# Other start addresses in SBUF for the weights and for the tiles that are multiplied with them

## The chip, the cores and the metric

The kernel runs on one core of a Trainium2 chip. The metric is the time of one execution on the device in microseconds (us). Three runs of the kernel before took 629.53, 631.18 and 634.5 us; their median is 631.18 us.

## The reference

Causal attention over 4 batches, 12 heads, 448 positions and a head size of 64, and behind it a layer of two matrices with a hardswish between them, on all 1792 positions. All is float32.

```python
scores = (1 / sqrt(64)) * matmul(q, k^T); scores = where(above diagonal, -1e9, scores)
attn = exp(scores - max); attn = attn / (sum(attn) + 1e-9)
x = heads of matmul(attn, v), side by side            # (1792, 768)
h = x @ w_in                                          # w_in  (768, 2048)
g = h * clip(h + 3, 0, 6) / 6
out = g @ w_out                                       # w_out (2048, 768)
```

## The kernel before

The 1792 positions are worked on in four groups of 448 columns. For each group attention gives x, transposed, as six tiles of 128 rows by 448 columns; the layer then computes h (16 tiles of 128 x 448) and out (6 tiles).

A float32 number is split into a high part, rounded to the type fp32r, and a low part, the remainder. One product of 128 x 128 weights with a 128 x 448 tile is then three matmuls, written in `triple` (lines 670 to 672): high weights with high data (L670), high weights with low data (L671), low weights with high data (L672). Each loads its own 128 x 128 weights first (the records named LDWEIGHTS) and then streams 448 columns past them. Weights are read from the tiles `wh` (high) and `wl` (low), in the last stage partly from `pr2`. The streamed operand is called the moving operand here. In the first product of each group, and in everything of the last stage, it is a tile of the pool `d` of shape [128, 2, 448], the high part in the first 1792 bytes of each partition and the low part in the next 1792. In the second product of the first two groups it is one of the 16 slots of `gh` (high) or `gl` (low), 1792 bytes each.

Groups 0 and 1 are computed one after the other (`group`), with the attention of later groups run in between. Groups 2 and 3 are computed together in the last stage (`last_first`, `last_second`) by a scheme with seven instead of eight block products, whose sums and differences DVE, POOL and ACT make. The attention's own products (L357, L414, L427, L500, L523 and L594 in plain float32, L502 and L503 in fp32r) lie in the first 400 us.

The order of the instructions on all engines is made by a planner in Python (`Flow`), which simulates the engines with fixed costs and does not know addresses. Every tile is then taken from a pool of equal slots, one pool per tag. The pools are laid out one behind the other in SBUF in the order of the table `BUFS`, so that the size of each pool decides where the next one starts:

```text
pool, start in bytes per partition, slot size x slots, start of a slot modulo 512
gh      21024  28672 x 1    32 (slot i of 1792 bytes: 32 for even i, 288 for odd i)
gl      49696  28672 x 1    32 (the same)
prow    78368     64 x 4
r       78624   1792 x 4    288, 32
kl      85792   1792 x 3    288, 32
vr      91168   2048 x 3    32
wh      97312   3072 x 3    32
wl     106528   3072 x 3    32
pr2    115744   1536 x 3    32
pr1    120352    896 x 3
wd     123040   4096 x 6    160
d      147616   3584 x 22   160 (high part); 1792 further on 416 (low part)
```

A weight tile of 128 columns is 512 bytes wide, so every 128 x 128 piece of `wh`, `wl` or `pr2` starts at the same address modulo 512. Lines 225 to 229 make the pools. `move` (L268) and `minus` (L280) are the helpers through which ACT, DVE and POOL make the high and low parts.

Of the kernel before, what the change touches and what calls it, by code (L numbers as in the profile page):

```python
# [9 lines left out]
F32 = mybir.dt.float32  # L10
# [28 lines left out]
    gh=1, gl=1, prow=4, r=4, kl=3, vr=3, wh=3, wl=3, pr2=3, pr1=3, wd=6, d=22,  # L39
)  # L40
BANKS = dict(b=8)

KINDS = dict(
    qk="d qk", op="d op", x="d x", pt="d pt", pr3="d pr3", xq="d xq", xc="d xc", gt="d gt", so="d so",
# [172 lines left out]
def tile_causal_attention_hardswish_moe(ctx: ExitStack, tc: tile.TileContext, q, k, v, w_in, w_out, out):  # L217
# [4 lines left out]
    kept_s = nc.dram_tensor("kept_s", (4, 2, 2, 128, HK, 256), F32).ap()  # L222
    kept_x = nc.dram_tensor("kept_x", (2, NPAIR, 128, S), F32).ap()

    pools = {}
    for tag, bufs in dict(const=1, **BUFS).items():
        pools[tag] = ctx.enter_context(tc.tile_pool(name=tag, bufs=bufs))
    for tag, bufs in BANKS.items():
        pools[tag] = ctx.enter_context(tc.tile_pool(name=tag, bufs=bufs, space=bass.MemoryType.PSUM))

    flow = Flow({**BUFS, **BANKS, **MOST})

# [849 lines left out]
```

## Time and profile before

| | |
|---|---|
| median of three runs | 631.18 us |
| the profiled execution, its own time | 632.49 us |
| its span, first to last instruction | 630.8 us |
| TensorE (PE) busy | 611.4 us, 97% |
| DVE, ACT, POOL busy | 502.7, 366.7, 279.9 us |
| mean granted TensorE clock | 0.984 of full speed |

A matmul's record begins when it starts and ends when its result is modelled to have left the array, so records of neighbouring matmuls overlap and their durations say nothing of the rate. The rate of TensorE is read from the starts: the time from the start of one matmul to the start of the next, called the pace here. The rows give starts to 0.01 us, so a pace is taken over many matmuls.

### The profile page before, as it was taken

The numbers are of one execution on the slowest core, as the hardware profiler recorded it, in microseconds if no ns is written. First come the engines' busy times: TensorE is split into PE (matmuls) and PEld (weight loads), VectorE is DVE, ScalarE is ACT, GpSimd is POOL, SyncE is SP. The second block draws the span as 40 slices with busy tenths as digits, with TensorE's granted clock in tenths as the row PEclk, the third lists the DMA queues.
The fourth block names the chain that finished last, engine by engine and source line by source line (L and its number), as shares of the span: only waits on it lengthen the run. The fifth ranks groups of instructions, "written<-read, shape, count | busy, mean of one in ns | idle before, by whom it ended". The sixth has DMA issues, their size and how long they took to land.

```text
span 630.8 us, 11229 instructions
## 1 busy us (share of the span) xinstructions
PE 611.4 (97%) x3636; PEld 526.7 (83%) x3636; DVE 502.7 (80%) x1060; ACT 366.7 (58%) x861; POOL 279.9 (44%) x274
## 2 busy tenths in 40 slices
PE   6879999999999999999999999999999999999997
PEld 5659797887887878779888788899999989999996
DVE  4998988897798665786998887498878888798851
ACT  3766666655545757667677655375555465446630
POOL 1667686464444434459377553015654453010000
PEclk8869999999999999999999999999999999999999
DMA  9979887787898444466477664335455367583311
GB/s 224 238 243 321 267 268 248 242 263 263 289 302 249 137 132 149 128 173 178 133 199 210 190 176 129 122 113 178 155 155 163 117 189 237 155 264 101 123 55 55
DMA packets 83578, 118.81 MB, mean 188 GB/s; under 512 B 22272, under 2 KB 59328, under 8 KB 83520
## 3 DMA queue, kind: packets, MB, share of 16 engines
q1 hardware_dynamic: 83520, 118.10, 61.7%
q8 instruction: 29, 0.48, 0.3%
q14 instruction: 29, 0.24, 0.1%
HBM read 90.93 MB, written 27.13 MB: 187 GB/s over the span
## 4 chain that ended last, share of the span: by engine, by line
PE 87%; DVE 5%; DMA 4%; SPq 1%; issue 1%; ACT 1%; POOL 0%; ACTq 0%; DVEq 0%
PE b L670 23%; PE b L672 22%; PE b L671 22%; PE b L523 7%; PE b L594 6%; PE b L500 5%; DMA gl<-in_v_dram 2%; DMA gh<-in_k_dram 1%; SPq L259 1%; PE b L502 1%; DVE d L280 1%; PE b L503 1%; DVE kl L280 1%; DVE b L555 1%; DVE gl L280 0%
## 5 line engine op out<-in xcount | busy, mean ns | idle before, releaser
L670 PE MATMUL b<-d,wh 128*128 128x448 f32 x504 | 189.3, 376 | 1.4 <-ACT r L268 1.1
L672 PE MATMUL b<-d,wl 128*128 128x448 f32 x504 | 185.1, 367 | 0.0
L671 PE MATMUL b<-d,wh 128*128 128x448 f32 x504 | 184.8, 367 | 0.0
L268 ACT CAST wh<-wd 128x768 fp32r<-128x768 f32 (+1 forms) x92 | 71.5, 778 | 59.5 <-PE b L671 39.1
L670 PEld LDWEIGHTS b<-d,wh 128*128 128x128 f32 x504 | 95.3, 189 | 11.7 <-ACT r L268 1.4
L672 PEld LDWEIGHTS b<-d,wl 128*128 128x128 f32 x504 | 95.1, 189 | 8.2
L671 PEld LDWEIGHTS b<-d,wh 128*128 128x128 f32 x504 | 95.3, 189 | 7.4
L280 DVE TENSOR_TENSOR wl<-wd,wh 128x768 fp32r<-128x768 f32 (+1 forms) x65 | 61.6, 947 | 30.2 <-ACT wh L268 30.0
L555 DVE CUSTOM_DVE_ANT_0 b<-b,mask 112x448 f32<-112x448 f32 (+2 forms) x144 | 69.7, 533 | 19.5 <-PE b L500 14.0
L280 POOL TENSOR_TENSOR wl<-wd,wh 128x768 fp32r<-128x768 f32 (+1 forms) x27 | 47.1, 1747 | 69.4 <-ACT wh L268 63.1
L268 ACT COPY d<-b 112x336 f32<-112x336 f32 (+3 forms) x137 | 55.7, 452 | 36.2 <-PE b L594 26.6
L280 POOL TENSOR_TENSOR wl<-d,wh 128x512 fp32r<-128x512 f32 (+1 forms) x38 | 58.2, 1534 | 39.8 <-ACT wh L268 37.6
L670 PE MATMUL b<-gh,wh 128*128 128x448 f32 x192 | 73.5, 383 | 0.0
L672 PE MATMUL b<-gh,wl 128*128 128x448 f32 x192 | 70.2, 365 | 0.0
L671 PE MATMUL b<-gl,wh 128*128 128x448 f32 x192 | 70.1, 365 | 0.0
L562 ACT ACTIVATE pr<-b,prow 112x336 f32<-112x336 f32 (+1 forms) x96 | 46.9, 495 | 7.7 <-PE b L594 4.8
L280 POOL TENSOR_TENSOR wd<-wd 128x256 f32<-128x256 f32 (+1 forms) x20 | 19.9, 1001 | 57.6 <-DMA wd<-kept_w 34.2
L523 PE MATMUL b<-d,vr 112*64 112x224 f32 (+2 forms) x504 | 44.9, 329 | 0.0
L523 PEld LDWEIGHTS b<-d,vr 112*64 112x64 f32 x504 | 30.6, 137 | 15.5 <-issue 2.8
L594 PE MATMUL b<-ident,pr 112*112 112x112 f32 x240 | 41.1, 261 | 0.0
L582 POOL TENSOR_SCALAR pr<-pr,prow 112x224 f32<-112x224 f32 (+1 forms) x52 | 27.6, 540 | 29.9 <-DVE prow L575 24.9
L268 ACT CAST wh<-d 128x512 fp32r<-128x512 f32 (+1 forms) x40 | 28.3, 707 | 21.6 <-DVE d L647 9.7
(116 smaller groups left out, 1157.2 us busy)
## 6 DMA issues: line engine op xcount, KB each, us to landing
wd<-in_w_in_dram SPq DMA_DIRECT2D x32, 384.0 KB, 5.1
wd<-in_w_out_dram SPq DMA_DIRECT2D x24, 512.0 KB, 5.4
wd<-kept_w SPq DMA_DIRECT2D x32, 384.0 KB, 3.4
wd<-kept_w SPq DMA_DIRECT2D x84, 128.0 KB, 3.1
d<-in_k_dram SPq DMA_DIRECT2D x72, 112.0 KB, 3.0
kept_w<-d SPq DMA_DIRECT2D x16, 384.0 KB, 5.4
kept_w<-d SPq DMA_DIRECT2D x24, 256.0 KB, 5.4
wd<-kept_w SPq DMA_DIRECT2D x24, 256.0 KB, 2.9
```

The lines of the kernel that those rows point to most:

```text
L259: flow.op(key, {"SP": (1, 0)}, [(0.1, lambda e: nc.sync.dma_start(out=o(), in_=i()), w)], r, nbytes=nbytes)
L268: nc.scalar.copy(o(), i()) if scale is None else nc.scalar.mul(o(), i(), scale)
L280: (nc.gpsimd if e == "P" else nc.vector).tensor_tensor(o(), a(), b(), op)
L500: nc.tensor.matmul(dst, ap(qk[0])[m, c], ap(qk[0])[m, nq:nq + w], start=True, stop=True)
L523: nc.tensor.matmul(ap(av)[64 * e:64 * e + 64, off + nq - w:off + nq], ap(vr)[:, j, e, :], ap(ph)[:, e, o:o + w], start=(j == 0), stop=(j = ...
L555: lambda _, e=e, i=i, w=w, dst=dst, st=st: nc.vector.tensor_tensor_reduce(dst(), dst(), mask[:, S - w:], -0.125, 3.0e38, ALU.add, ALU.min, ...
L562: lambda _, e=e, i=i, dst=dst, st=st, pr=pr: nc.scalar.activation(row_of(pr, e, i), dst(), ACTF.Exp, bias=ap(st)[:, e, i:i + 1], scale=-1. ...
L582: (nc.gpsimd if w == "P" else nc.vector).tensor_scalar(x, x, ap(st)[:, e, 4 + i:5 + i], 1.0, ALU.mult, ALU.mult)
L594: nc.tensor.transpose(ap(tp)[:C, C * o:C * o + C], row_of(pr, e, i)[:, C * j:C * j + C], ident)
L670: nc.tensor.matmul(ps, ap(wh)[:, a], xh, start=start, stop=False, skip_group_check=more)
L671: nc.tensor.matmul(ps, ap(wh)[:, a], xl, start=False, stop=False, skip_group_check=more)
L672: nc.tensor.matmul(ps, ap(wl)[:, a], xh, start=False, stop=stop, skip_group_check=more)
```

## The change

Ahead of the pool `wh` and ahead of the pool `d` a pool of one tile of 112 float32 numbers per partition (448 bytes) is opened. Nothing writes or reads these two tiles.

```diff
@@ -39,6 +39,7 @@
 BANKS = dict(b=8)
+SHIFT = dict(wh=112, d=112)

@@ -222,8 +223,11 @@
     pools = {}
     for tag, bufs in dict(const=1, **BUFS).items():
+        if tag in SHIFT:
+            ctx.enter_context(tc.tile_pool(name=f"shift_{tag}", bufs=1)).tile([128, SHIFT[tag]], F32, name=f"shift_{tag}")
         pools[tag] = ctx.enter_context(tc.tile_pool(name=tag, bufs=bufs))
```

The pools `wh`, `wl`, `pr2`, `pr1` and `wd` move up by 448 bytes and `d` by 896; all pools ahead of `wh` stay. The order of the instructions on every engine, their shapes, their waits and the slot of its pool that each tile takes are the same in both programs; only addresses differ. Of the 2160 matmuls of `triple`, 1584 have both operands moved (weights by 448, moving operand by 896) and 576 (those with `gh` and `gl`) the weights alone.

```text
start modulo 512                     before         after
weights in wh, wl, pr2               32             480
moving operand in d, high / low      160 / 416      32 / 288
moving operand in gh, gl             32 / 288       32 / 288

moving start minus weights' start, modulo 512
products with d, high / low          128 / 384      64 / 320
products with gh, gl, even / odd     0 / 256        64 / 320
```

## Rows read from the trace of the kernel before

**Rows 1.** The page: span, and busy time of each engine.

```profile
span 630.8 us, 11229 instructions
PE 611.4 (97%) x3636; PEld 526.7 (83%) x3636; DVE 502.7 (80%) x1060; ACT 366.7 (58%) x861; POOL 279.9 (44%) x274
```

**Rows 2.** The page: the chain that ended last, shares of the span by engine.

```profile
PE 87%; DVE 5%; DMA 4%; SPq 1%; issue 1%; ACT 1%; POOL 0%; ACTq 0%; DVEq 0%
```

**Rows 3.** Stages: start:end, length, busy us and count by engine, clock, DMA share, GB/s.

```profile
50.00:130.00 80.00, 80.00 (x472) 66.97 (x470) 71.10 (x162) 52.16 (x125) 56.99 (x55) 1.00 0.84 272
...
331.00:401.00 70.00, 68.57 (x497) 59.24 (x497) 56.43 (x145) 43.18 (x112) 33.20 (x32) 1.00 0.58 170
401.00:517.00 116.00, 116.00 (x573) 106.56 (x569) 94.21 (x151) 64.22 (x109) 52.26 (x39) 1.00 0.49 150
517.00:631.00 114.00, 108.68 (x532) 99.66 (x531) 83.64 (x132) 52.69 (x90) 10.16 (x8) 1.00 0.46 142
```

**Rows 4.** TensorE groups of instructions by shape: count, busy us, mean ns, idle before.

```profile
L670 PE MATMUL b<-d,wh 128*128 128x448 f32 x504 | 189.3, 376 | 1.4 <-ACT r L268 1.1 <-ACT kl L268 0.3
...
L670 PE MATMUL b<-gh,wh 128*128 128x448 f32 x192 | 73.5, 383 | 0.0
...
L670 PE MATMUL b<-d,pr 128*128 128x448 f32 x24 | 8.8, 365 | 0.0
```

**Rows 5.** Timeline of TensorE: start us, us; 188 matmuls with `d` in unbroken sequence.

```profile
519.79 0.37 PE L672 MATMUL b<-d,wl 128*128 128x448 f32 x1
519.99 0.37 PE L670 MATMUL b<-d,wh 128*128 128x448 f32 x1
...
557.94 0.36 PE L670 MATMUL b<-d,wh 128*128 128x448 f32 x1
```

**Rows 6.** The same view, 71 matmuls with `gh` and `gl` in unbroken sequence.

```profile
401.80 0.36 PE L672 MATMUL b<-gh,wl 128*128 128x448 f32 x1
...
415.99 0.36 PE L670 MATMUL b<-gh,wh 128*128 128x448 f32 x1
```

**Rows 7.** The same view: attention's 224-column matmuls, then twelve with `gh` and `gl`.

```profile
330.58 0.27 PE L502 MATMUL b<-d 128*112 128x224 f32 x1
...
330.99 0.38 PE L670 MATMUL b<-gh,wh 128*128 128x448 f32 x1
...
331.41 0.37 PE L672 MATMUL b<-gh,wl 128*128 128x448 f32 x1
...
333.27 0.36 PE L672 MATMUL b<-gh,wl 128*128 128x448 f32 x1
```

**Rows 8.** The same view: attention's fp32r matmuls of 448 columns, operands in `d` and `kl`.

```profile
342.08 0.37 PE L503 MATMUL b<-kl,d 128*112 128x448 f32 x1
342.29 0.37 PE L502 MATMUL b<-d 128*112 128x448 f32 x1
...
342.90 0.36 PE L503 MATMUL b<-kl,d 128*112 128x448 f32 x1
343.10 0.36 PE L594 MATMUL b<-ident,pr 112*112 112x112 f32 x2
```

**Rows 9.** Timeline of the weight loads in that stretch: start us, us.

```profile
330.58 0.18 PEld L503 LDWEIGHTS b<-kl,d 128*112 128x112 f32 x1
330.69 0.17 PEld L502 LDWEIGHTS b<-d 128*112 128x112 f32 x1
330.79 0.17 PEld L503 LDWEIGHTS b<-kl,d 128*112 128x112 f32 x1
```

**Rows 10.** Groups by shape: two of DVE's, whose operands lie in moved pools.

```profile
L280 DVE TENSOR_TENSOR wl<-wd,wh 128x768 fp32r<-128x768 f32 x48 | 49.0, 1020 | 18.8 <-ACT wh L268 18.7
...
L280 DVE TENSOR_TENSOR d<-gh,d 128x448 fp32r<-128x448 f32 x34 | 22.8, 695 | 0.6 <-ACT d L268 0.6
```

## The prediction

> **What bounds the kernel now.** I read the page first. TensorE is busy 97% of the span and no other engine above 80% [rows 1]; 87% of the chain that ended last is TensorE's own work [rows 2]. The table of stages says where: from 50 us on TensorE is busy all of the time, or nearly, at the full granted clock, and in the last 230 us, where every product is one of `triple`, DVE has 94.2 of 116 us and 83.6 of 114 us to do [rows 3]. So TensorE's own pace sets the end, and a nanosecond per matmul is worth a nanosecond per matmul, as long as the others keep up.
>
> How much hangs on that pace is a count: L670 stands in the trace 504, 192 and 24 times [rows 4], L671 and L672 as often, which makes (504 + 24) x 3 = 1584 matmuls with a moving operand in `d` and 192 x 3 = 576 with `gh` and `gl`.
>
> The pace itself is read from starts. With `d`, 187 steps take 557.94 - 519.79 = 38.15 us, 204.0 ns each [rows 5]. With `gh` and `gl`, 70 steps take 14.19 us, 202.7 ns each [rows 6]. In another place the same matmuls with `gh` and `gl` go more slowly: 9 steps from 331.41 to 333.27, 206.7 ns each [rows 7]. The granted clock is full, 1.00, in the stages that hold them [rows 3]. 448 columns at 2.4 GHz, one per tick, would be 186.7 ns, so 16 to 20 ns of every matmul go to something else, and that something comes in at least three sizes. This is the only place that I can find where addresses could count for the end of the program: all else that the change moves lies beside TensorE's work.
>
> **The change, part by part.** It adds no instruction, wait or transfer, removes none and moves none. What is left is the price of addresses, and there are four kinds of access to price.
>
> Weight loads. They begin with the matmul ahead of them and are recorded with 0.17 to 0.19 us, but that isn't what sets the pace: in the 224-column stretch one starts every 0.10 us, each recorded with 0.17 us [rows 9], and the matmuls there follow each other at (330.99 - 330.58) / 4 = 102.5 ns [rows 7]. The loads overlap there. Price of their new addresses by themselves: nothing, while they stay that short of the bound.
>
> The moving operand, and its place against the weights that are loaded meanwhile. The 102.5 ns for 224 columns are 0.458 ns per column, the 204.0 ns for 448 columns 0.455 ns. The loss is proportional to the columns streamed, although nearly the same weights are loaded in half the time. A collision between the two reads should have cost about as much per load, that is twice as much per column in the short matmul. That speaks against the idea that the two streams stand in each other's way, and so against a large effect of their relative address. What the address may still do is the difference between the stretches. I bound it by the nearest rows:
> - After the change the moving operands in `d` start at 32 and 288 modulo 512, as `gh` and `gl` do. If the moving operand's own address decides, `d` goes at the pace of [rows 6]: 1584 x (202.7 - 204.0) = -2.1 us, and `gh` keeps its own.
> - If the distance to the weights decides, the trace has two neighbours. L502 at 224 columns has its moving operand 320 bytes past its weights, one of the two distances that the change gives to everything; the four matmuls from 330.58, two of which are of that kind, scale to 205 ns for 448 columns [rows 7]. L502 at 448 columns has 448 bytes, 64 short of a full turn; five steps from 342.08 to 343.10 make 204.0 ns [rows 8]. With 205 for everything: 1584 x 1.0 + 576 x 2.3 = +2.9 us.
>
> The ends are -2.1 and +2.9 us. The start times have a grain of 0.01 us, 2% of a stretch of four short matmuls, so the second end is the weaker one; I take 203.2 ns for all, between [rows 6] and [rows 8] and nearer to the first: 1584 x (-0.8) + 576 x 0.5 = -1.0 us.
>
> The Trainium skill says the same from another side: by "SBUF — State Buffer", section "Who interferes with whom", TensorE waits for no other reader of SBUF, and its two read ports are independent. By that rule the change would be worth 0 us. The three paces of [rows 5 to 7] differ by 2% at one clock and one shape, so something beyond that rule acts on the stream, though no row says that it is the address.
>
> DVE, ACT and POOL. Two of DVE's large groups have operands in moved pools: 48 subtractions of 1020 ns and 34 of 695 ns [rows 10]. In the first, weights in `wd` and `wh` both move by 448, so their distance is the same; in the second only one side moves. If the 34 changed by a tenth it would be 34 x 70 ns = 2.4 us of DVE time, and in [rows 3] DVE has 22 and 30 us of slack in the two last stages. Price 0, hidden by TensorE's stream; with that cover gone 2.4 us at most, either way.
>
> DMA. The landing places of `wd` and `d` move by multiples of 64 bytes; the DMA share is 0.49 and 0.46 in the last stages and 0.84 at its highest in [rows 3], and nothing in the chain but the first 4% waits for it [rows 2]. Price 0.
>
> Sum: -1.0 us. The profiled execution took 632.49 us with a span of 630.8 us; it lies 1.3 us above the median of the three runs, 631.18 us. On that median the sum gives 630.2, so 630 us, with an own range of 626 to 635 us: inside 1% of 631.18 (624.9 to 637.5), which is about what a measurement of this kernel tells from no change.
>
> **The rivals.**
>
> *The reads do collide, and the new distance ends it.* All products before have distances that are multiples of 128 bytes, all after lie 64 beside one. If SBUF is cut in pieces that are taken in turn, a shift by half a step could free the stream where multiples of 128 couldn't. For it: 17.3 ns of every matmul with `d` and 16.0 with `gh` have no other name in the profile, and the pace differs between distances of 128 and 384 [rows 5] and 0 and 256 [rows 6]. Against it: the loss per column in 224-column matmuls, and L502's 204 to 205 ns at distances that are odd multiples of 64 [rows 7, 8]. If half the loss went, at some 195.3 ns: 1584 x 8.7 + 576 x 7.4 = 18.0 us, so 613 us; if all of it went, at 186.7 ns, 36.6 us, so 595 us. DVE would not stop it: two last stages shortened by 5% leave 110 and 108 us for its 94.2 and 83.6 us [rows 3]. It is faster by over 1% once the mean pace falls by 6.3 us / 2160 = 2.9 ns, from 203.7 to 200.8.
> The Trainium skill's "TensorE: Matmul & The Clock Gate", section "Wait — 56ns, not 53.3ns?", has back-to-back bfloat16 matmuls start every N / 2.4 GHz plus 2.5 ns. For 448 columns that would be 189.2 ns, an estimate from that page, and 31 us less for 2160 matmuls. The rows here show 202.7 to 206.7 ns in fp32r, so the trace disagrees with it for this type.
>
> *The slow pace becomes the rule.* The pace of 206.7 ns [rows 7] exists today at distances of 0 and 256, beside 202.7 ns at the same distances: the stream settles in one or the other. If the new distances let it settle in the slow one everywhere, 1584 x 2.7 + 576 x 4.0 = +6.6 us, 638 us. For it: nothing but its existence, and that the 224-column rows scale to 205. Against it: in the stretches that I read it lasts for some ten matmuls at a time, and the long stretches show the other two. It decides from a mean of 206.6 ns on, and each further nanosecond costs 2.2 us.
>
> *The change does nothing at all*, because the two tiles get no room of their own: excluded, since the start addresses of the pools differ in the built program as the table shows. That it changes addresses and no pace is part of my forecast.
>
> **How the numbers follow.** The forecast, a pace within 1.5% of today's, has 0.47: the rows at the nearest distances say so, but they are few and short. The freed stream has 0.33, the slow pace 0.20; the three sizes of pace at one shape keep me from going lower with either. The chances of faster by over 1%, within 1% and slower by over 1% are these three. For eight in ten the range reaches into both rivals: down to 610 us (a mean pace of about 194 ns, just beyond the half-freed stream; 0.08 is left below) and up to 641 us (about 208 ns; 0.06 above).
>
> **What would show it.** In the trace of the changed kernel, the starts in the last 110 us: 203 ns a step says forecast, 200 or less the freed stream, 206 or more the slow pace. If the paces with `d` and with `gh` become equal, the address decides as I worked it out, by the one or by the other reading; if they stay at 204.0 and 202.7 ns, it is not the address that tells them apart. DVE's 1020 and 695 ns should stay within a few per cent, and the chain should name TensorE with 85% or more. I am wrong if the span moves while the pace does not (then another engine's access had a price that I set to 0), or if the pace with 112-column weights in [rows 8] changes with the large ones, which would make the distance rather than the column count the cause of the loss.

## The result, and the profile after

The changed kernel takes 626.36 us (median of 9 runs, 623.43 to 629.28) against 631.18 us (9 runs, 628.28 to 634.91): a ratio of 0.9909, 95% interval 0.9882 to 0.9936. That is 0.9% faster by the ratio; the two medians lie 4.8 us apart, 0.8%. It is inside the range on record (610 to 641 us) and inside what the forecast called within 1%, at its faster end; the interval reaches beyond that end. The sum had said -1.0 us.

The page of the changed kernel has the span, the engines' busy time and the chain [as rows 1, 2]. Line numbers are higher by 4 from here on: `triple` is L674 to L676.

```profile
span 626.4 us, 11229 instructions
PE 605.9 (97%) x3636; PEld 526.6 (84%) x3636; DVE 503.1 (80%) x1060; ACT 367.1 (59%) x861; POOL 280.7 (45%) x274
PE 81%; DVE 6%; DMA 5%; issue 3%; POOL 2%; SPq 2%; ACT 1%; POOLq 0%; DVEq 0%; ACTq 0%
```

TensorE is still the bound: from 401 to 515 us it is busy 113.70 of 114 us. Its timeline, in the places of [rows 5 to 8], shows what changed (start us, us, instruction). A start in this kernel is not at the same time as its twin before; the stretches are chosen for being unbroken.

```profile
330.57 0.27 PE L506 MATMUL b<-d 128*112 128x224 f32 x1
...
330.99 0.37 PE L674 MATMUL b<-gh,wh 128*128 128x448 f32 x1
...
331.61 0.36 PE L674 MATMUL b<-gh,wh 128*128 128x448 f32 x1
...
333.20 0.37 PE L676 MATMUL b<-gh,wl 128*128 128x448 f32 x1
...
403.74 0.36 PE L675 MATMUL b<-gl,wh 128*128 128x448 f32 x1
...
415.94 0.36 PE L676 MATMUL b<-gh,wl 128*128 128x448 f32 x1
...
519.69 0.36 PE L675 MATMUL b<-d,wh 128*128 128x448 f32 x1
...
557.88 0.36 PE L674 MATMUL b<-d,wh 128*128 128x448 f32 x1
```

With `d`, 191 steps from 519.69 to 557.88 make 200.0 ns each, where [rows 5] had 204.0. With `gh` and `gl`, 61 steps from 403.74 to 415.94 make 200.0, where [rows 6] had 202.7. The stretch that went at 206.7 ns in [rows 7] has 8 steps in 1.59 us from 331.61 on, 199 ns within the grain of the starts. Three paces have become one. The four 224-column matmuls ahead of it take 0.42 us, against 0.41 in [rows 7]. In two of them (L506) both operands lie in `d` and keep their distance, 64 modulo 256; in the other two (L507, weights in `d`, moving operand in `kl`) it goes from 192 to 64 by the start addresses, so that now all four have it, and they are no faster.

**Where the microseconds came from.** The two programs run the same matmuls in the same order, so one can be followed through both. These are the starts of five of them, first in the kernel before (the third, at 401.80, is in [rows 6]), then in the changed one:

```profile
52.23 0.37 PE L672 MATMUL b<-d,wl 128*128 128x448 f32 x1
...
213.18 0.36 PE L670 MATMUL b<-d,wh 128*128 128x448 f32 x1
...
517.45 0.47 PE L670 MATMUL b<-d,wh 128*128 128x448 f32 x1 [0.35 <-ACT kl L268]
...
625.67 0.36 PE L672 MATMUL b<-d,wl 128*128 128x448 f32 x1
```

```profile
53.25 0.36 PE L676 MATMUL b<-d,wl 128*128 128x448 f32 x1
...
213.35 0.36 PE L674 MATMUL b<-d,wh 128*128 128x448 f32 x1
...
401.54 0.36 PE L676 MATMUL b<-gh,wl 128*128 128x448 f32 x1
...
515.17 0.48 PE L674 MATMUL b<-d,wh 128*128 128x448 f32 x1 [0.47 <-ACT kl L272]
...
621.29 0.36 PE L676 MATMUL b<-d,wl 128*128 128x448 f32 x1
```

| stretch of the kernel before | us before | us after | difference | matmuls of `triple` in it |
|---|---|---|---|---|
| 0 to 52.23 | 52.2 | 53.3 | +1.0 | 32 |
| 52.23 to 213.18 | 160.95 | 160.10 | -0.85 | 556 |
| 213.18 to 401.80 | 188.62 | 188.19 | -0.4 | 476 |
| 401.80 to 517.45 | 115.65 | 113.63 | -2.0 | 565 |
| 517.45 to 625.67 | 108.22 | 106.12 | -2.1 | 531 |

In the last two stretches the pace is the whole story: 70 steps by 2.7 ns and 495 by 4.0 make 2.2 us, 530 by 4.0 make 2.1 us. In the two before, attention's work breaks the runs of products into short pieces, and of some 3.5 us by the same reckoning 1.3 arrive. The pieces of 16 and more steps go at 199.9 to 200.4 ns there too, so what is missing lies between such pieces and not in their pace. One place where gain is given back can be read. In the timeline of the changed kernel TensorE reaches a group of transposes (L598) at 327.02 us, 0.29 earlier than before (327.31), and starts the third of them at 328.61, where it had started it at 328.60, because it waits for DVE to scale their input in both. The first line is of the kernel before, the other two are of the changed one:

```profile
328.60 0.31 PE L594 MATMUL b<-ident,d 112*112 112x112 f32 x1 [0.94 <-DVE d L582]
```

```profile
327.02 0.26 PE L598 MATMUL b<-ident,pr 112*112 112x112 f32 x1
...
328.61 0.31 PE L598 MATMUL b<-ident,d 112*112 112x112 f32 x1 [0.25 <-DVE d L586]
```

The +1.0 us of the start lies where TensorE waits for its first inputs: in the first 42 us the DMA engines moved 220 GB/s in the profiled execution before and 198 GB/s in this one. But that is not all of it: the fourth experiment below moved 221 GB/s and reached the first of the five matmuls later still. Over the profiled executions of all kernels of this document that matmul starts between 49.08 us (experiment 5) and 55.13 us (experiment 4). I take the +1.0 us for the scatter of single executions; nothing shows that the addresses do it.

### The profile page after: what moved, and what is told of

Its sections match the earlier page's. It is cut to its first block, busy times and chain, and to the rows that moved or that the text cites. A ratio compares the mean times of both kernels' runs of the same rounds, so it can differ in the third digit from the quotient of the medians.

```text
span 626.4 us, 11229 instructions
## 1 busy us (share of the span) xinstructions
PE 605.9 (97%) x3636; PEld 526.6 (84%) x3636; DVE 503.1 (80%) x1060; ACT 367.1 (59%) x861; POOL 280.7 (45%) x274
## 4 chain that ended last, share of the span: by engine, by line
PE 81%; DVE 6%; DMA 5%; issue 3%; POOL 2%; SPq 2%; ACT 1%; POOLq 0%; DVEq 0%; ACTq 0%
PE b L674 21%; PE b L675 20%; PE b L676 20%; PE b L527 7%; PE b L598 6%; PE b L504 5%; DMA gl<-in_v_dram 3%; SPq L263 2%; DMA gh<-in_k_dram 2%; PE b L506 1%; PE b L507 1%; DVE kl L284 1%; DVE b L648 1%; DVE b L646 1%; POOL wl L284 1%
## 5 line engine op out<-in xcount | busy, mean ns | idle before, releaser
L674 PE MATMUL b<-d,wh 128*128 128x448 f32 x504 | 187.0, 371 | 1.5 <-ACT r L272 1.1
L675 PE MATMUL b<-d,wh 128*128 128x448 f32 x504 | 182.8, 363 | 0.0
L676 PE MATMUL b<-d,wl 128*128 128x448 f32 x504 | 182.1, 361 | 0.0
L674 PEld LDWEIGHTS b<-d,wh 128*128 128x128 f32 x504 | 94.7, 188 | 11.0 <-ACT r L272 1.3
L676 PEld LDWEIGHTS b<-d,wl 128*128 128x128 f32 x504 | 94.4, 187 | 6.6
L674 PE MATMUL b<-gh,wh 128*128 128x448 f32 x192 | 73.0, 380 | 0.0
L676 PE MATMUL b<-gh,wl 128*128 128x448 f32 x192 | 69.7, 363 | 0.0
L598 PE MATMUL b<-ident,pr 112*112 112x112 f32 x240 | 41.5, 262 | 0.8 <-DVE pr L586 0.8
```

The lines of the kernel that those rows point to most:

```text
L598: nc.tensor.transpose(ap(tp)[:C, C * o:C * o + C], row_of(pr, e, i)[:, C * j:C * j + C], ident)
L674: nc.tensor.matmul(ps, ap(wh)[:, a], xh, start=start, stop=False, skip_group_check=more)
L675: nc.tensor.matmul(ps, ap(wh)[:, a], xl, start=False, stop=False, skip_group_check=more)
L676: nc.tensor.matmul(ps, ap(wl)[:, a], xh, start=False, stop=stop, skip_group_check=more)
```

## The experiments

Each kernel is the changed one with another table `SHIFT` (in float32 numbers; 16 of them are 64 bytes). Ratios are against the kernel before, run again beside each group of experiments (medians 631.92 us for 1 to 4, 632.11 for 5 to 8, 632.68 for 9 and 10), with 95% intervals. The granted clock is 1.00 in all the stretches named. Every fence is the timeline of TensorE. A distance is given modulo 512 with its two values, or modulo 256 with one.

**1. All pools up, all distances as before.**

```diff
-SHIFT = dict(wh=112, d=112)
+SHIFT = dict(gh=112)
```

> One stretch of 448 bytes ahead of gh alone: all pools from gh on move by 448, so the weights start at 480 modulo 512 as in the change, gh/gl at 480 and 224, d at 96 and 352, and every distance between moving operand and weights is that of before (0/256 and 128/384). Theory A (the distance decides the pace): 204.0 ns per matmul with d and 202.7 with gh/gl as before, time within 2 us of before. Theory B (the weights' own address decides): 200.0 ns for both, time 4 to 5 us below before.

0.9993 (0.9969 to 1.0017), no change.

```profile
403.67 0.37 PE L674 MATMUL b<-gh,wh 128*128 128x448 f32 x1
...
415.86 0.37 PE L676 MATMUL b<-gh,wl 128*128 128x448 f32 x1
...
519.74 0.36 PE L675 MATMUL b<-d,wh 128*128 128x448 f32 x1
...
557.88 0.37 PE L676 MATMUL b<-d,wl 128*128 128x448 f32 x1
```

187 steps with `d` make 204.0 ns, as before, though the weights start at 480 as in the change. Theory B falls. With `gh` and `gl`, 59 steps make 206.6 ns: the slow pace of [rows 7], this time for a whole stretch. At 128.4 us the same kernel ran 40 steps of them at 202.7. So at a distance of 0 and 256 two paces are possible, at the same start addresses modulo 512, and theory A's 202.7 for `gh` and `gl` came in one stretch and not in the other.

**2. The weights where they were, all distances as in the change.**

```diff
-SHIFT = dict(wh=112, d=112)
+SHIFT = dict(gh=16, wh=112, d=112)
```

> Stretches of 64 bytes ahead of gh, 448 ahead of wh, 448 ahead of d: the weights start at 32 modulo 512 as before, the moving operands at 96 and 352, so all distances are 64 and 320 as in the change. Theory A (distance): 200.0 ns for both kinds, time 4 to 5 us below before. Theory B (the weights' own address): 204.0 and 202.7 ns, time as before.

0.9899 (0.9859 to 0.994; 4 runs), faster by what the change is.

```profile
403.71 0.36 PE L674 MATMUL b<-gh,wh 128*128 128x448 f32 x1
...
415.91 0.36 PE L675 MATMUL b<-gl,wh 128*128 128x448 f32 x1
...
519.64 0.36 PE L674 MATMUL b<-d,wh 128*128 128x448 f32 x1
...
557.84 0.36 PE L676 MATMUL b<-d,wl 128*128 128x448 f32 x1
```

61 and 191 steps, 200.0 ns both. Theory A holds: with other addresses for every operand, the distance alone brings the pace of the change.

**3. The first stretch alone.**

```diff
-SHIFT = dict(wh=112, d=112)
+SHIFT = dict(wh=112)
```

> The first stretch alone (448 bytes ahead of wh): distance 64/320 for gh/gl, 128/384 as before for d, the weights at 480. Theory A (distance): 200.0 ns with gh/gl, 204.0 with d, time 1 to 1.5 us below before (576 x 2.7 ns). Theory B (weights' own address): 200.0 for both, 4 to 5 us below.

0.9973 (0.995 to 0.9997), 630.03 us.

```profile
403.72 0.36 PE L675 MATMUL b<-gl,wh 128*128 128x448 f32 x1
...
415.92 0.36 PE L676 MATMUL b<-gh,wl 128*128 128x448 f32 x1
...
519.73 0.37 PE L675 MATMUL b<-d,wh 128*128 128x448 f32 x1
...
557.88 0.37 PE L676 MATMUL b<-d,wl 128*128 128x448 f32 x1
```

200.0 ns with `gh` and `gl` (61 steps), 204.0 with `d` (187 steps): theory A, and 1.7 us by the ratio (0.2 to 3.2) where it expected 1 to 1.5.

**4. A stretch ahead of `d` alone.**

```diff
-SHIFT = dict(wh=112, d=112)
+SHIFT = dict(d=112)
```

> A stretch of 448 bytes ahead of d alone: distance 64/320 for d, 0/256 as before for gh/gl, weights at 32 as before. Theory A (distance): 200.0 ns with d, 202.7 with gh/gl, time 3 to 5 us below before. Theory B (weights' own address): 204.0 and 202.7, time as before. Theory C (the moving operand's own address in d): 200.0 only if 96/352 does what 32/288 did; 204.0 otherwise.

0.9924 (0.9894 to 0.9953), 626.55 us.

```profile
403.76 0.36 PE L675 MATMUL b<-gl,wh 128*128 128x448 f32 x1
...
415.92 0.36 PE L675 MATMUL b<-gl,wh 128*128 128x448 f32 x1
...
519.74 0.36 PE L674 MATMUL b<-d,wh 128*128 128x448 f32 x1
...
557.94 0.36 PE L676 MATMUL b<-d,wl 128*128 128x448 f32 x1
```

The mirror image: 202.7 ns with `gh` and `gl` (60 steps), 200.0 with `d` (191 steps). Most of the gain is here, as most of the matmuls are. Theory C falls with experiment 1: there `d` starts at 96 and 352 as here, and goes at 204.0. Experiments 1 to 4 together leave the distance: each kind of product goes at a pace of its own distance, and in none of them did an operand's own address count.

**5 to 7. Other distances.**

```diff
-SHIFT = dict(wh=112, d=112)
+SHIFT = dict(wh=56, d=16)       # experiment 5
+SHIFT = dict(wh=40, d=8)        # experiment 6
+SHIFT = dict(wh=16, d=24)       # experiment 7
```

> Distances 288/32 for gh/gl and 192/448 for d (stretches of 224 and 64 bytes). Theory A1 (the pace goes by the distance modulo 128: 0 is bad, 64 is good): d 200.0 ns as in the change; gh/gl, at 32 modulo 128, between 200.0 and 204; time 4 to 5 us below before. Theory A2 (modulo 256, where 64 is a lucky place and 192 another): d anything from 196 to 207, each ns off 200.0 worth 1.6 us.

0.996 (0.9941 to 0.9979), 629.27 us.

```profile
150.79 0.36 PE L675 MATMUL b<-gl,wh 128*128 128x448 f32 x1
...
157.74 0.37 PE L676 MATMUL b<-gh,wl 128*128 128x448 f32 x1
...
403.74 0.36 PE L674 MATMUL b<-gh,wh 128*128 128x448 f32 x1
...
415.94 0.36 PE L675 MATMUL b<-gl,wh 128*128 128x448 f32 x1
...
519.73 0.37 PE L675 MATMUL b<-d,wh 128*128 128x448 f32 x1
...
557.95 0.37 PE L675 MATMUL b<-d,wh 128*128 128x448 f32 x1
```

`d` at 192 and 448 goes at 202.2 ns (189 steps), not at 200.0: theory A1 falls, 64 and 192 are not the same. With `gh` and `gl`, at 288 and 32, one stretch goes at 204.4 ns (34 steps) and another at 200.0 (61 steps): again two paces at one distance.

> Distances 352/96 for gh/gl and 160/416 for d (stretches of 160 and 32 bytes): 96 and 32 modulo 128. Theory A1 (modulo 128): both equal what a distance of 32 or 96 gives, 200.0 to 204 ns, time between that of the change and that of before. Theory A2 (modulo 256): d and gh/gl need not agree with the 32 of the run beside it.

0.9975 (0.9946 to 1.0004), 630.24 us, not clear of no change. Here products with `d`, at one and the same distance, change their pace within a run:

```profile
424.75 0.36 PE L675 MATMUL b<-d,pr 128*128 128x448 f32 x1
...
450.35 0.36 PE L674 MATMUL b<-d,wh 128*128 128x448 f32 x1
...
513.98 0.47 PE L674 MATMUL b<-d,wh 128*128 128x448 f32 x1 [0.47 <-ACT kl L272]
...
519.66 0.37 PE L674 MATMUL b<-d,wh 128*128 128x448 f32 x1
...
557.89 0.37 PE L676 MATMUL b<-d,wl 128*128 128x448 f32 x1
```

With `d` at 160 and 416, 128 steps from 424.75 make 200.0 ns, and the pace is the same up to 513.15; then TensorE waits 0.47 us, until 513.98, for ACT, and behind that wait 185 steps make 206.7. The distance offers two paces. That the wait chose the other is not shown: the next stage begins at the same place, and the changed kernel has the same wait at 515.17 and keeps its pace. `gh` and `gl` at 352 and 96 go at 205.4 ns, with no second pace seen.

> Distances 448/192 for gh/gl and 224/480 for d (stretches of 64 and 96 bytes). Theory A1 (modulo 128): gh/gl 200.0 ns as at 64; d, at 96 modulo 128, as the gh/gl of the run at 96. Theory A2 (modulo 256): gh/gl at 192 as the d of the run at 192, whatever that is, and not bound to 200.0.

1.0006 (0.9979 to 1.0032), no change from before.

```profile
403.71 0.36 PE L675 MATMUL b<-gl,wh 128*128 128x448 f32 x1
...
415.85 0.36 PE L675 MATMUL b<-gl,wh 128*128 128x448 f32 x1
```

`gh` and `gl` at 448 and 192 go at 202.2 to 202.3 ns (60 steps), which is the 202.2 of `d` at that distance in experiment 5, and `d` at 224 and 480 at 204.4 (187 steps from 519.69 to 557.92). So modulo 128 is excluded, and the pace is the same for both kinds of product: theory A2. That 256 is the period and not 512 rests on one comparison. Every stream here mixes two distances that lie 256 apart, two to one with `d` and half and half with `gh` and `gl`; that both mixes of 192 and 448 go at 202.2 says that these two count alike.

**8. A shorter weight load.**

```diff
-        a = slice(128 * c, 128 * c + 128)
+        a, b = slice(128 * c, 128 * c + 128), slice(128 * c, 128 * c + 96)
...
-        nc.tensor.matmul(ps, ap(wh)[:, a], xl, start=False, stop=False, skip_group_check=more)
+        nc.tensor.matmul(ps[:96], ap(wh)[:, b], xl, start=False, stop=False, skip_group_check=more)
```

> The addresses of the change, but the second matmul of every three (high weights, low data) takes 96 of its 128 weight columns and so leaves a quarter of its result out; its load reads 384 bytes for 512. Theory D (what is left of the loss, 13.3 ns over 448 columns at one per tick, is a collision with the weight load and goes by the bytes loaded): the steps in which that load runs fall by a quarter of 13.3, so the mean pace falls from 200.0 to about 198.9 ns. Theory E (the loss goes by the columns streamed, as the 224-column matmuls suggested): the pace stays 200.0 ns.

```profile
519.68 0.36 PE L676 MATMUL b<-d,wl 128*128 128x448 f32 x1
...
557.88 0.36 PE L675 MATMUL b<-d,wh 128*96 128x448 f32 x1
```

191 steps, 200.0 ns, as theory E expected and not D's 198.9. It ran once, 629.15 us, so no time is compared. In other stretches (46 steps from 153.7 us, 58 from 81.7) the pace is 204.5 ns, one that this distance did not show with full loads. The short loads are indeed shorter, 161 ns on record against 186 to 188 for the others, and in the stretch shown three steps still make 600 ns, as in the changed kernel. So a quarter less to load in one of three gains nothing there, and elsewhere the stream was slower with it; whether the load does that or one of several paces came by, a single execution does not tell. That the 13.3 ns that are left of each matmul go by the bytes of weights, as theory D had it, falls.

**9 and 10. Steps of 16 bytes around the distance of the change.** The slots of `wh` and `wl` get 832 numbers instead of 768, and the weights start 4 (experiment 9) or 60 (experiment 10) numbers into them. The weights in `pr2`, 72 of the 2160 matmuls, all between 421 and 518 us, keep the distance of the change, so that stage is left out of the table for 48 and 80.

```diff
+            if b.tag in ("wh", "wl"):
+                b.tile = pools[b.tag].tile([128, 832], b.dt, tag=b.tag, name=b.tag)[:, 4:4 + 768]
+                return b.tile
             b.tile = pools[b.tag].tile(b.shape, b.dt, tag=b.tag, name=b.tag)
```

> The stretches of the change, and the slots of wh and wl 256 bytes longer with the weights 16 bytes into them, so that the moving operand starts 48 bytes past its weights modulo 256, for d and gh/gl alike. Theory G (the pace is a smooth function of the distance with its best place near 64): 200 to 201 ns, time within 1 us of the change. Theory H (it changes from one 16-byte step to the next): anything from 196 to 207 ns, each ns worth some 2 us.

1.0004 (0.9977 to 1.0031).

```profile
519.71 0.37 PE L679 MATMUL b<-d,wl 128*128 128x448 f32 x1
...
557.94 0.37 PE L677 MATMUL b<-d,wh 128*128 128x448 f32 x1
```

> The same with the weights 240 bytes into their slots: distance 80 modulo 256 for d and gh/gl alike. Theory G (smooth): between the 200.0 ns of a distance of 64 and the 205.3 of 96, some 202 to 203 ns, time 4 to 7 us above that of the change. Theory H (from step to step): anything from 196 to 207 ns.

0.9998 (0.9964 to 1.0033).

```profile
519.81 0.36 PE L677 MATMUL b<-d,wh 128*128 128x448 f32 x1
...
557.83 0.37 PE L678 MATMUL b<-d,wh 128*128 128x448 f32 x1
```

204.4 and 203.3 ns (187 steps each). 16 bytes either way lose the whole gain in time. Theory G falls at 48; theory H, which allowed anything from 196 to 207 ns, is what is left. All paces seen in unbroken stretches of 16 and more steps, from the starts:

| distance modulo 256 | ns per matmul of 448 columns |
|---|---|
| 0 | 202.2 to 202.8, at times 205.9 to 206.7 |
| 32 | 200.0, 204.4 or 206.6 |
| 48 | 203.9 to 204.4 |
| 64 | 200.0, shorter stretches 199.9 to 200.8, in all 4 kernels with full loads that have it |
| 80 | 203.1 to 203.6, at times 206.7 |
| 96 | 205.1 to 205.4 |
| 128 | 204.0, shorter stretches 203.3 to 204.1, once 206.7 |
| 160 | 200.0 to 200.3, or 206.7 |
| 192 | 201.9 to 202.5 |
| 224 | 204.4, shorter stretches 203.2 to 204.6 |

In the long stretches no distance went below 200.0, and none but 64 kept to it. Six of the sixteen multiples of 16 were not tried. No version is faster than the changed kernel by more than the intervals.

A pace is the mean of a pattern. The trace keeps starts in whole nanoseconds, and in them the steps with `d` between 425 and 513 us repeat: 202, 201, 197 in the changed kernel, which is three matmuls and 600 ns, and 209, 196, 204, 211, 200 in the kernel before, which is five matmuls and 1020 ns. With five, each of the three matmuls of `triple` meets every step in turn, so the pace there does not come from one of the three.

## Why the prediction was right, and where its steps were off

**The bound** was right. Of the 4.4 us between the two spans the two last stretches of the table make 4.1, where TensorE's pace sets the end, and there a nanosecond per matmul was worth a nanosecond per matmul. One sign of it that the prediction named did not come: the chain names TensorE with 81% and not with 85%. In the last stages that is a matter of its route. Followed back from the end, it leaves TensorE at the wait at 515.17 us for ACT, DMA and POOL, while TensorE is busy all but 0.3 us from 401 to 515 us.

**The sum** had the right sign and a fifth of the size, since its term for the pace, "203.2 ns for all", was mis-sized: it measured 200.0. Two of its rows misled. The first bound took the moving operand's own address as the cause; in experiments 1, 3 and 4 `d` starts at the same 96 and 352 and goes at 204.0, 204.0 and 200.0 ns, so it is not that. The second took the 224-column matmuls of [rows 7] and L502 in [rows 8] as neighbours of the new distance. They are not: the first had it in two of four steps only, and with all four at it they are no faster in the changed kernel; neither is an unbroken run, while experiments 5 and 6 show that a stream can settle in more than one pace. With 200.0 ns the same sum would have been 1584 x 4.0 + 576 x 2.7 = 7.9 us; the measured ratio is worth 4.0 to 7.4 us, and the trace shows the missing part in the first 400 us, where the products come in short runs. That the time stayed within 1% was in part luck: 7.9 us would have been 1.25% of 631.18, and the prediction had no term for what the two stretches before 402 us gave back, 2.2 of some 3.5 us.

**That the two reads don't stand in each other's way** was wrong as put. The argument, that the loss goes by the columns and not by the load, agrees with experiment 8. But "so against a large effect of their relative address" does not follow from it: the distance between the moving operand and the weights moves the pace between 200.0 and 206.7 ns, 3.3%, with load and columns the same.

**The rival of the freed stream** had the right variable, the distance, and the wrong size. By the prediction's own sign, 200 ns or less in the last 110 us, it is what came; and that the paces with `d` and with `gh` became equal was the sign that the address decides. It asked for half of the loss; 4.0 of 17.3 ns went. That the two reads collide is not shown, only that their distance sets the pace. The mean pace passed the 200.8 ns from which it was to be faster by over 1%, and the median did not, for the gain that the attention stages lost. Its picture of pieces taken in turn, in which every odd multiple of 64 would do, fell in experiments 5 and 7, where 192 gave 202.2.

**The rival of the slow pace** has a real pace behind it: 206.6 ns over 59 steps in experiment 1 and 206.7 over 185 in experiment 6. It did not come at the distance of the change, in any stretch of the four kernels that have it with full loads.

**The rule** of the Trainium skill's "SBUF — State Buffer", section "Who interferes with whom", that TensorE waits for no other reader of SBUF and has two independent read ports, gave 0 us. About other engines no run here says anything against it. For TensorE's own two reads the runs do: in experiment 2 the weights stand where they stood modulo 512, only the moving operands and so the distance are new, and 1% is gained.

**DVE** at price 0 was right, and for **DMA** no run shows a price. The two groups of [rows 10] have the same means in the changed kernel, 1020 and 694 ns:

```profile
L284 DVE TENSOR_TENSOR wl<-wd,wh 128x768 fp32r<-128x768 f32 x48 | 49.0, 1020 | 17.3 <-ACT wh L272 17.2
...
L284 DVE TENSOR_TENSOR d<-gh,d 128x448 fp32r<-128x448 f32 x34 | 22.8, 694 | 0.6 <-ACT d L272 0.6
```

**The last sign of being wrong** could not decide. Five steps of the matmuls of [rows 8] take 1.03 us in the changed kernel and took 1.02, but with `d` moved and `kl` not, L507 goes from 64 to 192 modulo 256 and L506 keeps 192, so neither got the distance of the change.

**What stays open**: by what mechanism the distance acts, whether it counts to the weights in use or to those that are loaded meanwhile (both start at one address modulo 256 here), why modulo 256, why some distances allow two or three paces and what chooses among them, and what the 13.3 ns per matmul are that no distance removed. Part of the gain that fell short between 52 and 402 us was not followed to its waits.

## What to carry to other kernels

Where a long stream of matmuls sets the end, read the pace from starts over some hundred of them, and compare it between stretches that differ in nothing but their tiles; a difference of 1% there is a lead and not noise. Padding between pools is a cheap thing to try, but sweep it: here 64 bytes modulo 256 gained 2% of pace with `d`, and 48 and 80 gained nothing in time. A few matmuls in a row are no bound for a stream of hundreds.

## What the runs showed of the hardware that I had not expected

- The pace of an fp32r stream of 448 columns depends on the distance between the moving operand and the weights in SBUF, modulo 256 bytes, between 200.0 and 206.7 ns at full granted clock (1.00); an effect of an operand's own address was not seen (experiments 1 to 7, 9 and 10).
- At some distances it has more than one steady pace: 200.0 ns before and 206.7 ns behind a wait of 0.47 us, at a distance of 160 and 416 (experiment 6). What chooses is not shown.
- A weight load of 96 instead of 128 columns in one matmul of three does not make the stream faster; in one execution it went at 200.0 ns in some stretches and at 204.5 in others (experiment 8).
